# Block-sparse attention and a low-rank mixer on one core: another written-out order of steps, a refilled prologue, and w2 loaded around the values of pair 7

## The chip, the cores and the metric

The kernel runs on one core of one Trainium2 chip. The metric is the device time of one execution in microseconds (us), the median of several runs; lower is better. TensorE is called PE here, VectorE DVE, ScalarE ACT, GpSimd POOL and SyncE SP, as the profile does. DVE, ACT, POOL and SP each run their own instructions in program order, and so does PE.

## The reference: what is computed

There are two stages. The first is attention with a block mask, for 4 batches of 8 heads, 768 positions and 64 channels:

```python
scores = scale * np.matmul(q, k.transpose(0, 1, 3, 2))      # scale = 1/8
mask = np.abs(blk_i - blk_j) <= window                      # blocks of 32, window 1
mask = mask | (blk_i == 0) | (blk_j == 0) | (blk_i == n_blocks - 1) | (blk_j == n_blocks - 1)
for qb in range(n_blocks):
    for kb in sampled_blocks[qb]:                           # three random key blocks
        mask[qb * block:(qb + 1) * block, kb * block:(kb + 1) * block] = True
attn = softmax(np.where(mask, scores, -1000000000.0))
out = np.matmul(attn, v)
```

The mask is the same for all heads. The second stage takes the heads' outputs side by side as x (4 batches of 768 positions by 512 channels), mixes positions with a product of rank 32, and runs a two-layer perceptron over the channels:

```python
u = x + (x.transpose(0, 2, 1) @ U @ V).transpose(0, 2, 1)   # U 768x32, V 32x768
out = u + np.maximum(u @ w_ch1, 0.0) @ w_ch2                # 512 -> 2048 -> 512
```

## The kernel before

**Units of work.** The 32 heads are 16 pairs; pair i belongs to batch i // 4. Queries, keys and values come in as float32 and are used as 16-bit floats. A score is computed with the 128 keys of a tile as output rows and the 768 queries as columns; ACT takes the exponential of it out of PSUM into the tile `est`, with no maximum subtracted. A value product multiplies `est` by the values, which carry a column of ones, so that the sum of the exponentials comes out as a 65th column; DVE divides by it.

**Pairs 0 to 3 (batch 0).** The mask rides along in the product: `qres` and `kres` hold the 64 channels of a head and, in other rows, a one-hot code of the query's block and a row of biases for the key, so the score comes out already masked. A single score (`score`, L980) is two matmuls of 384 columns into two banks of PSUM, with an exp of 768 columns (L989); a double score (`two_scores`, L999) is four matmuls into three banks, with an exp of 1536 columns (L1007). Meanwhile PE and DVE work out the mask as an array (`mask_part`, L939), tile by tile.

**Pairs 4 to 15.** Both heads of a pair share `qpl` and `kpl`, which a DMA transposes (`front`). A quad step (`two_halves`, L1030) computes two key tiles of both heads in eight matmuls into six banks; ACT does two exps of 1536 columns (L1039), and DVE multiplies each by the mask (L1045). The value products of a head are 36 matmuls of 65 columns (L414).

**The mixer** follows a batch later, between the scores of the next batch: the products with U and V (L572 to L665), the first layer with weights `w1t` (L685), its relus on ACT (L697) or DVE (L699), and the second layer with weights `w2t` (L760). The second layer is not the plain product: it is put together from seven products of quarter size (a scheme of Strassen's kind), for which DVE forms sums of the weights (`weight_sum`, L721 or L855 and about there) and of the hidden values (`pair_sum`), and adds the products into the result (`pair_out`, L879). For the last batch both layers are done in that way (L817 to L919).

**Banks.** PSUM has eight banks. A step that writes PSUM names the bank that it takes; a step may only write a bank when the reader of what was there is done.

**The order.** Nothing is scheduled by the framework: the kernel writes the order out by hand. First comes a prologue, in plain statements. Then one long string, `PLAN`, gives a word for each step, and the loop over `PLAN.split()` emits the instructions word by word; an engine's program is what falls to it, in that order. The words that matter here:

- `S3`: a single score into banks 3 and 4; `B0`: a double score into banks 0 to 2; `Q`: a quad step into banks 0 to 5; `H`: half of one; `e`: the next exp on ACT; `p`: the mask multiply on DVE.
- `A`, `A7`: one tile of a value product, the number naming the bank where a new one begins; `V6`: all six tiles of a head; `v`: the divide on DVE; `y`: the copy behind it.
- `Z7`, `z`: PE turns the second head of pair 0, DVE copies it; `R6`, `t`: the same for queries or keys of pairs 1 to 4; `K6`, `k`: a part of the mask array and the DVE compare behind it.
- `M`, `m`, `X`, `Y`, `D`, `d`, `E`, `g`, `F`, `x`, `d.`, `T.`: the mixing with U and V; `P`, `C`, `U`, `a`, `b`: the first layer and its relus; `S.`, `H.`, `D.`: the second layer's sums, products and additions; `q.`: sums of weights.
- `t.`, `g.`, `c.`, `o.`, `r.`, `s.`, `h.`, `e.`: the two layers of the last batch, the tail of the kernel.
- `L.n`: the loads of a later pair, from `loads(n + 1)`.

**The prologue.** Two loads of pair 0's first head go out; PE runs eight matmuls of 512 columns on a constant (`keep_warm`, L272), whose result nobody reads; DVE casts the queries and works out a small array `bias` from the sampled blocks; PE turns queries and keys (`first_turn`, L227) and multiplies out the two halves of the mask rows (`mask_half`, L279); DVE and ACT copy them into `qres` and `kres` (`mask_row` L287, `first_row` L293). Then POOL casts the second head and clears some tiles, and the first transfers of pairs 0 and 1, of U, of the second set of mask rows (`second_set`) and of V are issued.

**The loads.** `loads(i)` issues, on SP, the transposes of pair i + 1 (`front`), and, on POOL, in transfers that convert to 16 bits, the queries and keys of pair i + 2 (`load_qk`) and then its values (`load_v`), two transfers for each tensor of a pair from pair 6 on (L139). The earlier pairs come through SP's queue as float32 and are cast by POOL or, in pair 0, by DVE too. w2 comes in four quarters of four row blocks (`load_w2`, L372): two behind the values of pair 6, in `loads(4)`, and two behind those of pair 7, in `loads(5)`.

The functions that the diff touches, and those that call them:

Of the kernel before, what the change touches and what calls it, by code (L numbers as in the profile page):

```python
# [23 lines left out]
def kernel(  # L24
# [167 lines left out]
    def second_set():  # L192
        for h in range(2):
            one_hot(1, h)
            nc.sync.dma_start(out=kres[1][mrows[h], h, :], in_=kres[0][mrows[h], h, :])
        nc.sync.dma_start(out=kmask[mrows[0], :], in_=kres[0][mrows[0], 0, :])

    def load_mix_u():
        uld = ldpool.tile([P, T, R], FP32, tag="ldu", name="uld", bufs=1)
        nc.sync.dma_start(out=uld, in_=moe_U.rearrange("(p t) r -> p t r", t=T))  # L200
        nc.gpsimd.tensor_copy(out=Ut[:, :, 0:R], in_=uld)

# [30 lines left out]

    with tc.manual_schedule(
# [41 lines left out]
        pks = [bank(2, [P, HS], FP32), bank(7, [P, HS], FP32)]  # L276
# [23 lines left out]
        keep_warm(8)  # L300
# [28 lines left out]
        mask_row(0, 1, nc.vector.tensor_copy)  # L329
        mask_row(1, 1, nc.vector.tensor_copy)  # L330
# [3 lines left out]
        for tile_ in (Vt, kmask):  # L334
            nc.gpsimd.memset(tile_.bitcast(FP32), 0.0)
        nc.vector.memset(Ut, 0.0)
# [3 lines left out]
        load_mix_u()  # L340
        second_set()
# [107 lines left out]
    S0 S3 e e S5 B0 e Z7 e S3 z Z6 e z A7 A B0 e R6 S3 t A R5 e A B0 t A K6 e A S3 k v A5 A e K6 k B0 A  # L449
    A e K7 A K6 k S3 k A K7 e v B0 k S3 e M6 e A5 A m R7 A t B0 K6 R3 e k A A t S6 A e v S0 D2 S3 e d A7  # L450
    A e A S0 K6 A e S3 k K2 A e S5 k A e v S3 R2 e S5 t S0 e M7 e S3 m D2 e B5 d A0 D1 e A A d A S3 D2 A
    e d K1 S5 k R7 e S3 t A S1 e v A5 A e A S3 S6 e K2 A e A k A S3 v B0 e K7 M6 e k S3 m X5 K7 e A6 Y k
    A B0 y X7 Y e S3 y E5 A e A g A R7 S0 t A e v S4 S2 e A7 A e R1 E6 A t A g A A Q v e e M6 X7 m Y P6
    y p H U7 e p H b C e p H b U7 e p H b U6 e p E1 a g p V7 Q v e e V6 U7 v p U0 a P1 b C p P6 a C E7 Q
    a g U6 e e U7 b P6 b p U0 C a U7 p a Q b X6 Y e e P7 y C P6 b C p U0 b a p V7 L.5 Q v U.0.1.3.6 e
    q.3.0 V7 a.0.1.3.0 e U.0.1.1.1 v U.0.1.11.0 a.0.1.1.1 U.0.1.5.6 q.3.1 a.0.1.11.1 p Q a.0.1.5.1 p
    U.0.1.10.6 e U.0.1.7.7 a.0.1.10.0 e U.0.1.2.6 a.0.1.7.0 S.0.0.1.3 U.0.1.9.7 p a.0.1.2.1 Q a.0.1.9.1
    q.7.1 U.0.1.4.6 e S.0.0.2.0 H.0.0.1.0.7 p H.0.0.1.1 a.0.1.4.1 U.0.1.0.0 p L.6 e U.0.1.14.1 q.4.1 V6
    a.0.1.0.1 p a.0.1.14.1 Q v q.4.0 e V6 D.0.0.0 S.0.0.3 H.0.0.6.0 e v U.0.1.13.2 q.7.0 H.0.0.6.1
    U.0.1.12.6 a.0.1.13.1 D.0.0.2 y p Q a.0.1.12.1 q.5.1 H.0.0.7.0 e H.0.0.7.1 q.5.0 H.0.0.5.0.6 D.0.0.3  # L460
    H.0.0.5.1 e S.0.0.4.4 U.0.1.6.1 p H.0.0.4.0 a.0.1.6.1 H.0.0.4.1 D.0.0.4 Q D.0.0.5 p H.0.0.3.0 e L.7
    H.0.0.3.1 p H.0.0.2.0.7 H.0.0.2.1 e p U.0.1.8.2 U.0.1.15.0 D.0.0.1 D.0.0.6 a.0.1.8.1 V7 p a.0.1.15.1
    S.0.1.1.1 Q S.0.2.1.0 V6 e v S.0.1.2.4 H.0.1.1.0.7 y v H.0.1.1.1 y H.0.1.2.0.0 S.0.2.2.3 y H.0.1.2.1
    e D.0.1.0 M6 D.0.1.1 H.0.2.1.0.1 m H.0.2.1.1 S.0.2.3 F.1.0.2.4 D.0.2.0 F.1.1.3.6 F.1.2.5.0 x.6.0
    H.0.2.6.0 x.6.1 d.6.0 H.0.2.6.1 x.7.0 d.6.1 F.1.3.6.4 D.0.2.2 H.0.1.6.0 T.6 x.5.1 H.0.1.6.1 S.0.1.3
    H.0.2.7.0 H.0.2.7.1 x.4.0 H.0.2.5.0.6 x.5.0 H.0.2.2.0.0 D.0.2.3 d.5.0 H.0.2.2.1 x.4.1 d.5.1
    H.0.2.4.0 D.0.1.2 d.4.0 T.5 x.7.1 H.0.2.4.1 d.7.0 H.0.1.7.0 D.0.2.1 d.4.1 D.0.2.5 H.0.1.7.1 d.7.1
    S.0.2.4.2 T.4 Q D.0.1.3 H.0.2.5.1 e H.0.1.4.0 T.7 D.0.2.4 H.0.1.4.1 H.0.2.3.0 e D.0.1.5 H.0.2.3.1
    Z.0.0.1 p H.0.1.5.0.7 Z.0.2.1 H.0.1.5.1 D.0.2.6 Q Z.0.2.0 D.0.1.4 Z.0.0.0 S.0.1.4.0 U.1.0.0.6 e
    H.0.1.3.0 a.1.0.0.0 H.0.1.3.1 e U.1.0.11.6 D.0.1.6 p U.1.0.10.0 Z.0.1.0 Z.0.1.1 a.1.0.11.1 U.1.0.9.7  # L470
    p L.8 a.1.0.10.1 U.1.0.6.6 a.1.0.9.1 p Q a.1.0.6.1 p U.1.0.12.6 e V7 e U.1.0.2.2 v U.1.0.5.0 p
    a.1.0.12.1 U.1.0.1.7 a.1.0.5.1 a.1.0.2.1 U.1.0.3.6 a.1.0.1.0 p Q a.1.0.3.1 V6 p e U.1.0.4.7 v e
    U.1.1.5.2 a.1.0.4.0 U.1.0.15.6 p a.1.1.5.1 U.1.1.9.7 a.1.0.15.1 p Q a.1.1.9.1 U.1.1.3.7 e L.9
    U.1.0.7.6 a.1.1.3.0 e U.1.0.14.7 a.1.0.7.0 p U.1.1.4.0 U.1.1.10.6 a.1.0.14.1 a.1.1.4.0 U.1.1.1.7 p
    a.1.1.10.1 Q a.1.1.1.1 V7 e V6 v e U.1.1.7.7 v Q a.1.1.7.1 p U.1.0.8.7 e H.1.0.1.0.6 a.1.0.8.0
    H.1.0.1.1 p e U.1.1.13.7 p U.1.0.13.0 U.1.1.14.2 p a.1.0.13.1 a.1.1.13.1 U.1.1.8.3 S.1.0.1.3
    a.1.1.14.1 U.1.1.6.7 a.1.1.8.1 S.1.0.3 Q a.1.1.6.1 S.1.0.2.0 H.1.0.2.0.7 e D.1.0.0 L.10 H.1.0.2.1
    S.1.0.4.4 H.1.0.6.0 D.1.0.1 H.1.0.6.1 e U.1.1.15.1 U.1.1.11.0 a.1.1.15.0 U.1.1.0.7 p a.1.1.11.1 Q
    D.1.0.2 a.1.1.0.1 p y V7 e H.1.0.7.0 v e H.1.0.7.1 U.1.1.2.0 p U.1.1.12.7 D.1.0.3 a.1.1.2.1 p Q
    a.1.1.12.1 S.1.1.1.0 H.1.0.4.0 e H.1.0.4.1 S.1.1.2.1 V7 D.1.0.5 e S.1.1.3 H.1.1.1.0.6 p H.1.1.1.1 Q  # L480
    D.1.1.0 v H.1.1.6.0 e L.11 p H.1.1.6.1 H.1.0.5.0.7 D.1.1.2 H.1.0.5.1 e p H.1.1.7.0 H.1.1.7.1 D.1.0.4
    V0 y p y y H.1.1.5.0.3 S.1.1.4.3 y V4 y D.1.1.3 v H.1.1.5.1 v y H.1.1.4.0 H.1.1.4.1 S.1.2.1.1 y
    H.1.0.3.0 D.1.1.4 M4 S.1.2.2.0 H.1.0.3.1 m D.1.1.5 F.2.0.5.4 F.2.1.0.1 D.1.0.6 Z.1.1.1 H.1.2.1.0.6
    x.8.0 H.1.2.1.1 x.10.0 d.8.0 H.1.1.3.0 x.10.1 d.10.0 F.2.2.7.5 D.1.2.0 F.2.3.4.2 d.10.1 H.1.2.2.0.1
# [699 lines left out]
```

## Time and profile before

| what | us |
|---|---|
| median of three runs | 270.56 |
| the three runs | 269.94, 271.41, 270.56 |
| the profiled execution, its own time | 270.01 |
| its span in the profile | 268.2 |
| first exp on ACT | 6.54 |
| first exp of a quad step (pair 4) | 43.61 |
| w2's four transfers issued | 49.40, 50.14, 58.69, 62.78 |
| w2's four transfers landed | 58.41, 62.50, 71.13, 74.54 |

The page of the profile shows one execution. Its first lines give, for each engine, the time that it was busy, the share of the span and the number of instructions; PEld is the loading of weights, which runs beside the matmuls. A table by stretch gives the same for pieces of the span, and with it the TensorE clock that was granted (1.00 is full), the busy share of the DMA engines, and GB/s. A timeline lists the instructions of an engine in order of time, those alike put together: the start, the busy time, the engine, the line and the operation, out<-in with shapes, the count; a bracket at the end holds the idle time before it and what ended it. The chain of waits goes back from the last instruction to what released it, step by step, and gives the share of the span that falls to each engine. Times in a timeline are counted from the start of the span.

### The profile page before, as it was taken

Reading aid. Unit: us, or ns where it says so; the run is one execution under the profiler, and the core shown is the slowest. Engines: PE = TensorE matmul, PEld = TensorE weight load, DVE = VectorE, ACT = ScalarE, POOL = GpSimd, SP = SyncE. Lnnn points to the kernel's source line nnn. Section 1 sums busy time; section 2 is a strip of 40 time slices with the busy share of each in tenths; the row PEclk is TensorE's granted clock in tenths of the full one; section 3 lists DMA queues with packets and bytes.
Section 4 is the critical chain, followed back from the end, with each engine's and each line's share of the span. In section 5 each row is a group of like instructions: output and inputs, shape, how many; then the busy total and the mean of one; then the engine's idle time right before and its main releaser. Section 6 shows DMA issues by size and latency. Waiting matters only on the chain.

```text
span 268.2 us, 7303 instructions
## 1 busy us (share of the span) xinstructions
PE 262.4 (98%) x3006; PEld 182.4 (68%) x3006; DVE 232.5 (87%) x477; ACT 202.7 (76%) x265; POOL 72.7 (27%) x98
## 2 busy tenths in 40 slices
PE   8899999999999999999999999999999999999995
PEld 3677775555577778565666887555667788666884
DVE  5789988988999998868588997688998999999993
ACT  4999998897989667788898857788997944789200
POOL 4669006944462570070606160000000000000000
PEclk9999999999999999999999999999999999999999
DMA  6799997999999999897938997610200116400024
GB/s 192 245 324 263 207 235 123 113 135 144 189 146 133 117 103 111 284 98 89 90 39 67 106 109 139 223 34 13 51 0 2 42 42 117 159 2 0 2 98 137
DMA packets 88720, 31.66 MB, mean 118 GB/s; under 512 B 77104, under 2 KB 85840, under 8 KB 88688
## 3 DMA queue, kind: packets, MB, share of 16 engines
q0 software_dynamic: 49728, 10.10, 48.4%
q1 hardware_dynamic: 38492, 20.86, 33.6%
q8 instruction: 23, 0.38, 0.6%
q10 hardware_dynamic: 468, 0.26, 0.4%
q14 instruction: 9, 0.07, 0.1%
HBM read 27.67 MB, written 6.29 MB: 127 GB/s over the span
## 4 chain that ended last, share of the span: by engine, by line
PE 73%; DMA 12%; DVE 7%; ACT 2%; POOL 2%; issue 1%; SPq 0%; DVEq 0%; POOLq 0%; ACTq 0%
PE ps L760 32%; PE ps L685 17%; DMA w2t<-in_moe_w_ch_dram 9%; PE ps L414 9%; PE ps L1030 7%; DMA vld<-in_v_dram 2%; PE ps L999 2%; ACT est L1007 2%; PE ps L980 1%; DVE est L1045 1%; PE ps L272 1%; DMA qpl<-stqld 1%; PE ps L665 1%; DVE xf L551 1%; DVE res L969 1%
## 5 line engine op out<-in xcount | busy, mean ns | idle before, releaser
L1039 ACT ACTIVATE est<-ps 128x1536 f16<-128x1536 f32 x72 | 100.6, 1450 | 18.8 <-PE ps L1030 18.7
L685 PE MATMUL ps<-uT,w1t 128*128 128x384 f16 x384 | 70.2, 326 | 0.0
L1045 DVE TENSOR_TENSOR est<-est,mask 128x1440 f16<-128x1440 f16 x72 | 63.4, 903 | 0.6 <-ACT est L1039 0.2
L685 PEld LDWEIGHTS <-w1t 128*128 128x128 f16 x384 | 35.6, 97 | 26.6 <-issue 6.8
L414 PEld LDWEIGHTS <-est 128*128 128x128 f16 x1152 | 40.4, 97 | 7.0 <-issue 3.3
L414 PE MATMUL ps<-vt,est 128*128 128x65 f16 x1152 | 43.3, 193 | 0.2 <-DVE xf L551 0.2
L760 PEld LDWEIGHTS <-hid 128*128 128x128 f16 x358 | 34.0, 98 | 6.6 <-issue 1.6
L697 ACT ACTIVATE hid<-ps 128x384 f16<-128x384 f32 x63 | 29.7, 496 | 4.8 <-PE ps L685 4.3
L1030 PE MATMUL ps<-qpl,kpl 64*128 64x512 f16 (+1 forms) x288 | 31.7, 325 | 0.0
L139 POOL DMA_DIRECT2D stqld<-in_q_dram x20 | 16.3, 820 | 55.9 <-DMA qpl<-stqld 54.4
L760 PE MATMUL ps<-w2t,hid 128*128 128x256 f16 x238 | 31.1, 273 | 0.0
L879 DVE TENSOR_TENSOR xf<-xf,ps 128x256 f32<-128x256 f32 x63 | 25.4, 416 | 4.1 <-PE ps L760 3.7
L699 DVE TENSOR_SCALAR hid<-ps 128x384 f16<-128x384 f32 x33 | 18.3, 555 | 8.7 <-PE ps L685 8.0
L760 PEld LDWEIGHTS <-sums 128*128 128x128 f16 x216 | 20.1, 98 | 4.4 <-issue 1.0
L989 ACT ACTIVATE est<-ps 128x768 f16<-128x768 f32 x30 | 22.5, 812 | 0.1
L1030 PEld LDWEIGHTS <-kpl 64*128 64x128 f16 x288 | 12.3, 94 | 14.3 <-issue 9.1
L760 PE MATMUL ps<-res,sums 128*128 128x256 f16 x144 | 19.4, 273 | 0.0
L634 ACT CAST xh<-xf 128x384 f16<-128x384 f32 x24 | 11.0, 510 | 10.0 <-DVE xf L630 10.0
L551 DVE TENSOR_TENSOR xf<-ps,rcp 128x384 f32<-128x384 f32 x32 | 17.7, 554 | 0.8
L139 POOL DMA_DIRECT2D stkld<-in_k_dram x20 | 16.3, 819 | 1.9 <-issue 0.8
L139 POOL DMA_DIRECT2D vt<-in_v_dram x20 | 16.3, 820 | 0.0
L760 PE MATMUL ps<-res,hid 128*128 128x256 f16 x120 | 15.9, 273 | 0.0
(121 smaller groups left out, 339.3 us busy)
## 6 DMA issues: line engine op xcount, KB each, us to landing
out_dram<-xf SPq DMA_DIRECT2D x18, 256.0 KB, 2.4
vld<-in_v_dram SPq DMA_DIRECT2D x6, 384.0 KB, 6.3
w1t<-in_moe_w_ch_dram POOLq DMA_DIRECT2D x4, 512.0 KB, 8.3
w2t<-in_moe_w_ch_dram POOLq DMA_DIRECT2D x4, 512.0 KB, 12.1
qld<-in_q_dram SPq DMA_DIRECT2D x5, 384.0 KB, 3.7
kld<-in_k_dram SPq DMA_DIRECT2D x5, 384.0 KB
stqld<-in_q_dram POOLq DMA_DIRECT2D x20, 96.0 KB, 3.9
stkld<-in_k_dram POOLq DMA_DIRECT2D x20, 96.0 KB, 4.2
```

The lines of the kernel that those rows point to most:

```text
L139: nc.gpsimd.dma_start(out=dst[:, h], in_=src[b, 2 * hp + h].rearrange("(p t) d -> p t d", t=T),)
L414: nc.tensor.matmul(pav[:, sc, :], est[:, n, sc * P : (sc + 1) * P], vts[b % 2][:, 2 * hp + h, g, 0 : D + 1], start=(g == 0 and sc == 0), s ...
L551: nc.vector.tensor_tensor(out=dst, in0=pav[:, :, 0:D], in1=rcp[:, :, None].broadcast_to([P, T, D]), op=ALU.mult,)
L685: nc.tensor.matmul(pt, w1t[:, cc, jj * P : (jj + 1) * P], bts[b].uT[:, cc, c * HS : (c + 1) * HS], start=(cc == 0), stop=(cc == NCC - 1), ...
L697: nc.scalar.activation(out=dst, in_=pt, func=AF.Relu)
L699: nc.vector.tensor_scalar_max(out=dst, in0=pt, scalar1=0.0)
L760: nc.tensor.matmul(acc[key], lhsT, rhs, start=(first and i == 0), stop=(i == len(pairs_) - 1), skip_group_check=True,)
L879: nc.vector.tensor_add(out=x, in0=x, in1=acc[a, b, tau])
L989: lambda: nc.scalar.activation(out=dst, in_=ps, func=AF.Exp, scale=0.125),
L1030: nc.tensor.matmul(units[h][:, u * S + lo : u * S + hi], kT[drows[h], g * P : (g + 1) * P], qT[drows[h], lo:hi], start=True, stop=True, sk ...
L1039: nc.scalar.activation(out=both[h], in_=units[h].rearrange("p (g n) -> p g n", g=2), func=AF.Exp, scale=0.125,)
L1045: lambda: nc.vector.tensor_mul(out=masked(both[h]), in0=masked(both[h]), in1=masked(mask[:, 2 * j : 2 * j + 2, :]),),
```

## The change

There are three parts.

**The prologue.** `keep_warm` runs seven matmuls of 512 columns and one of 256, not eight of 512; three fillers of 128 columns are added, one ahead of the first mask step and two at the prologue's end. `first_turn` takes both halves of the turned tile as weights (128 columns, not 64), for which POOL sets the half that no load has filled to 1. A part of the first key turn's copy goes from ACT to DVE, the whole of the second key turn's from DVE to ACT. The second half of the mask, its three copies, the second set of rows and the load of V leave the prologue for a new word, `W7`, at the head of the list, where one of its rows' copies that ACT did is done by DVE. Some clearing of tiles moves on POOL, and that of `Ut` goes from DVE to POOL.

**The list.** `PLAN` is another list of the same steps: each kind of word is there as often as before, save for `W7`, each kind's own sequence is the same (for the dotted words of the mixer and the tail, their order is not), the relus are split between ACT and DVE in the same numbers, and many bank numbers differ.

**w2.** Its first half is issued behind the queries and keys of pair 7, its second behind that pair's values; `loads(0)` moves from the start of pair 0 to that of pair 1.

```diff
     def second_set():
         for h in range(2):
-            one_hot(1, h)
             nc.sync.dma_start(out=kres[1][mrows[h], h, :], in_=kres[0][mrows[h], h, :])
-        nc.sync.dma_start(out=kmask[mrows[0], :], in_=kres[0][mrows[0], 0, :])
+            if h == 0:
+                nc.sync.dma_start(out=kmask[mrows[0], :], in_=kres[0][mrows[0], 0, :])
...
-                pt[0:D, j * P : (j + 1) * P],
-                sts[0, ("qld", "kld")[n]][:, 3 * c + j, 0],
+                pt[:, j * P : (j + 1) * P],
+                sts[0, ("qld", "kld")[n]][:, 3 * c + j].rearrange("p h d -> p (h d)"),
...
+        for nm in ("qld", "kld"):
+            nc.gpsimd.memset(sts[0, nm][:, :, 1], 1.0)
         for tile_ in (qres[1], kres[1]):
             nc.gpsimd.memset(tile_.bitcast(FP32), 0.0)
-        for vt in vts:
-            nc.gpsimd.memset(vt[:, :, :, D : D + 1], 1.0)
...
-        pks = [bank(2, [P, HS], FP32), bank(7, [P, HS], FP32)]
+        pks = [bank(2, [P, HS], FP32)]
...
-        keep_warm(8)
+        keep_warm(7)
+        keep_warm(1, 256)
...
         first_row(0, 1, nc.scalar.copy)
+        keep_warm(1, P)
         first_cast(0, 1, nc.vector.tensor_copy)
         mask_half(0)
         mask_row(0, 0, nc.vector.tensor_copy, 0, P)
-        mask_row(1, 0, nc.scalar.copy)
         first_turn(1, 0)
         first_row(1, 0, nc.vector.tensor_copy, 0, P)
-        first_row(1, 0, nc.scalar.copy, P, HS)
         mask_row(0, 0, nc.vector.tensor_copy, P, HS)
+        first_row(1, 0, nc.vector.tensor_copy, P, HS)
         first_turn(1, 1)
-        first_row(1, 1, nc.vector.tensor_copy)
-        mask_half(1)
-        mask_row(0, 1, nc.vector.tensor_copy)
-        mask_row(1, 1, nc.vector.tensor_copy)
+        first_row(1, 1, nc.scalar.copy)
+        keep_warm(2, P)
...
+        for h in range(2):
+            one_hot(1, h)
+
+    def late_masks(n):
+        pks.append(bank(n, [P, HS], FP32))
+        mask_half(1)
+        for h, c in ((0, 1), (1, 0), (1, 1)):
+            mask_row(h, c, nc.vector.tensor_copy)
         second_set()
         load_mix_v()
...
     PLAN = """
-    S0 S3 e e S5 B0 e Z7 e S3 z Z6 e z A7 A B0 e R6 S3 t A R5 e A B0 t A K6 e A S3 k v A5 A e K6 k B0 A
+    W7 S0 S5 e e S3 B0 Z6 z Z5 z e e S6 B3 S1 e e e R6 t A7 A A A A A v B0 e K3 k A5 R6 A A K7 S3 e t B0 e
...
-    e d K1 S5 k R7 e S3 t A S1 e v A5 A e A S3 S6 e K2 A e A k A S3 v B0 e K7 M6 e k S3 m X5 K7 e A6 Y k
+    K1 k S5 e R7 t v S3 e S1 e A5 A A S3 S6 e K2 k A A A S3 e B0 e e v M7 m K6 k K5 k S3 e X7 Y y A6 A B0 X5
...
-    y p H U7 e p H b C e p H b U7 e p H b U6 e p E1 a g p V7 Q v e e V6 U7 v p U0 a P1 b C p P6 a C E7 Q
+    H C b p e p H U7 b e p H e U6 a E2 g V7 Q e e p v V6 v U7 a U0 b P1 C P6 C a a p p E7 g Q e e U6 b U7 P6
...
             load_qk(i + 2)
+            if i == HP + 1:
+                load_w2(range(0, NJJ // 2, 4))
             load_v(i + 2)
             if i == 1:
                 load_w1(range(NCC))
-        if i in (HP, HP + 1):
-            load_w2(range((i - HP) * NJJ // 2, (i - HP + 1) * NJJ // 2, 4))
+        if i == HP + 1:
+            load_w2(range(NJJ // 2, NJJ, 4))
...
-        for m in {0: (0,), 1: (1, 2), 3: (3,), 4: (4,)}.get(i, ()):
+        for m in {1: (0, 1, 2), 3: (3,), 4: (4,)}.get(i, ()):
             loads(m)
...
+        "W": ((late_masks,) for _ in range(1)),
```

More of the change, by code (lines that the diff above doesn't have):

```diff
@@ L320 @@
         mask_row(0, 0, nc.vector.tensor_copy, 0, P)
-        mask_row(1, 0, nc.scalar.copy)
         first_turn(1, 0)
         first_row(1, 0, nc.vector.tensor_copy, 0, P)
-        first_row(1, 0, nc.scalar.copy, P, HS)
         mask_row(0, 0, nc.vector.tensor_copy, P, HS)
+        first_row(1, 0, nc.vector.tensor_copy, P, HS)
         first_turn(1, 1)
-        first_row(1, 1, nc.vector.tensor_copy)
-        mask_half(1)
-        mask_row(0, 1, nc.vector.tensor_copy)
-        mask_row(1, 1, nc.vector.tensor_copy)
+        first_row(1, 1, nc.scalar.copy)
+        keep_warm(2, P)
         for n in range(2):
             first_cast(1, n, nc.gpsimd.tensor_copy)
-        for tile_ in (Vt, kmask):
-            nc.gpsimd.memset(tile_.bitcast(FP32), 0.0)
-        nc.vector.memset(Ut, 0.0)
+        for vt in vts:
+            nc.gpsimd.memset(vt[:, :, :, D : D + 1], 1.0)
+        nc.gpsimd.memset(kmask.bitcast(FP32), 0.0)
         load_v(0)
@@ L459 @@
[L459 to L478, printed above, removed]
@@ new lines @@
+    p p D.1.0.0 p U.1.1.8.7 a.1.1.8.1 U.1.0.13.1 a.1.0.13.1 S.1.0.1.3 S.1.0.2.0 S.1.0.4.4 U.1.1.14.2
+    a.1.1.14.1 U.1.1.13.5 a.1.1.13.1 U.1.1.6.7 a.1.1.6.1 Q e L.9 L.10 H.1.0.2.0.7 H.1.0.2.1 S.1.0.3
+    H.1.0.6.0 H.1.0.6.1 D.1.0.1 U.1.1.15.0 a.1.1.15.0 e p D.1.0.2 p U.1.1.11.1 a.1.1.11.1 U.1.1.0.7
+    a.1.1.0.1 Q e e V7 v y H.1.0.7.1 H.1.0.7.0 D.1.0.3 U.1.1.2.2 a.1.1.2.1 p p U.1.1.12.7 a.1.1.12.1
+    S.1.1.1.0 S.1.1.2.1 Q e e H.1.0.4.0 H.1.0.4.1 D.1.0.5 V7 S.1.1.3 p H.1.1.1.0.6 H.1.1.1.1 D.1.1.0 Q L.11
@@ new lines @@
+    U.2.0.10.6 a.2.0.10.0 p U.2.1.4.7 a.2.1.4.1 Q e e V7 v y U.2.1.0.6 a.2.1.0.0 U.2.1.2.1 a.2.1.2.0
+    U.2.0.1.7 a.2.0.1.1 U.2.0.13.6 a.2.0.13.1 Q e e p p U.2.1.9.7 a.2.1.9.0 U.2.0.7.6 a.2.0.7.0 U.2.0.6.7
+    a.2.0.6.1 U.2.0.14.6 a.2.0.14.1 L.12 L.13 Q e e p p V7 p V6 v y v U.2.0.3.7 a.2.0.3.1 S.2.0.1.4
+    S.2.0.2.1 Q e e U.2.1.5.6 a.2.1.5.0 S.2.0.3 H.2.0.1.0.7 H.2.0.1.1 D.2.0.0 U.2.1.14.0 a.2.1.14.1 y
+    U.2.1.10.1 a.2.1.10.0 p p p U.2.1.3.6 a.2.1.3.1 Q e e H.2.0.6.0 H.2.0.2.0.6 H.2.0.6.1 D.2.0.2 H.2.0.2.1
@@ L529 @@
+    e.2.6.1 e.2.6.0
     """
```

122 lines of the change are left out of this document (65 added, 57 removed).

## The prediction

> **What bounds the kernel now.** I read the page's sums first: TensorE is busy for nearly the whole span, and the chain of waits runs mostly through it.
>
> ```profile
> span 268.2 us, 7303 instructions
> PE 262.4 (98%) x3006; PEld 182.4 (68%) x3006; DVE 232.5 (87%) x477; ACT 202.7 (76%) x265; POOL 72.7 (27%) x98
> PE 73%; DMA 12%; DVE 7%; ACT 2%; POOL 2%; issue 1%; SPq 0%; DVEq 0%; POOLq 0%; ACTq 0%
> ```
>
> An average over the span hides the stages, so the second view is the table by stretch (busy us of PE, PEld, DVE, ACT and POOL, each with its instructions, then the granted clock).
>
> ```profile
> 6.50:43.60 37.10, 35.76 (x507) 26.14 (x507) 32.22 (x72) 34.21 (x39) 18.18 (x25) 1.00 0.96 246
> 52.20:80.00 27.80, 27.56 (x317) 17.05 (x317) 25.49 (x45) 22.94 (x27) 13.71 (x18) 1.00 1.79 154
> 80.00:206.00 126.00, 125.97 (x1529) 87.40 (x1525) 107.48 (x201) 101.06 (x123) 30.34 (x38) 1.00 0.87 97
> 228.00:265.00 37.00, 37.00 (x285) 27.57 (x282) 34.29 (x94) 18.90 (x41) 0.00 (x0) 1.00 0.17 61
> ```
>
> From 80 on PE idles 0.03 us in 126 and, in the tail, nothing at all: no order of steps can win there while the work is the same. Up to about 52 it is ScalarE: in its timeline each exp follows the last, except where a bracket shows idle time.
>
> ```profile
> 6.54 2.23 ACT L989 ACTIVATE est<-ps 128x768 f16<-128x768 f32 x3
> 8.68 1.45 ACT L1007 ACTIVATE est<-ps 128x1536 f16<-128x1536 f32 x1
> 10.03 0.81 ACT L989 ACTIVATE est<-ps 128x768 f16<-128x768 f32 x1
> 11.22 1.45 ACT L1007 ACTIVATE est<-ps 128x1536 f16<-128x1536 f32 x1 [0.39 <-PE ps L999]
> 12.57 0.81 ACT L989 ACTIVATE est<-ps 128x768 f16<-128x768 f32 x1
> 13.57 1.45 ACT L1007 ACTIVATE est<-ps 128x1536 f16<-128x1536 f32 x1 [0.20 <-PE ps L999]
> ...
> 43.61 8.16 ACT L1039 ACTIVATE est<-ps 128x1536 f16<-128x1536 f32 x6 [1.20 <-PE ps L1030]
> ```
>
> Starts are 0.71 us apart behind a 768-column exp, 1.35 behind a 1536-column one. The wait for L999 comes to 1.66 us in six gaps (0.39, 0.20, 0.20, 0.26, 0.26, 0.35): a double score written to banks 0–2 cannot begin before the double exp that reads them has ended. The 1.20 before 43.61 is the first quad score behind the last exp of pair 3; both lists have it. Last, the stretch in which w2 arrives:
>
> ```profile
> 74.63 0.69 DVE L721 TENSOR_TENSOR w2t<-w2t 128x1024 f16<-128x1024 f16 x1 [0.24 <-DMA w2t<-in_moe_w_ch_dram]
> 79.73 1.25 PE L414 MATMUL ps<-vt,est 128*128 128x65 f16 x36 [0.24 <-DVE xf L551]
> 49.40 1.52 POOL L372 DMA_DIRECT2D w2t<-in_moe_w_ch_dram  x2
> 58.69 0.75 POOL L372 DMA_DIRECT2D w2t<-in_moe_w_ch_dram  x1 [2.95 <-DMA w2t<-in_moe_w_ch_dram]
> 62.78 0.74 POOL L372 DMA_DIRECT2D w2t<-in_moe_w_ch_dram  x1 [3.34 <-DMA w2t<-in_moe_w_ch_dram]
> ```
>
> POOL issues the third quarter of w2 only when the first has landed (58.41), the fourth when the second has (62.50); the fourth lands at 74.54, and one weight sum on DVE waits 0.24 for it. PE's longest gap between two streams there is 0.40, just ahead of 79.73 (by the bracket 0.24, a divide on DVE).
>
> My base is the profiled execution: 270.01 us, its span 268.2 and 1.8 around it. It is 0.55 below the median of the runs, 270.56; I add my sum to the median.
>
> **The change, part by part.** The kinds and counts of the work are the same in both lists (48 A, 30 S, 9 B, 34 Q, 126 H with dots, 84 h, 63 relus on ScalarE and 33 on DVE). What changes is the prologue, the neighbours of each step, the bank numbers, and w2's place in POOL's queue.
>
> *Prologue.* The warming row is eight matmuls of 512 columns from 0.78 to 4.14, 427 ns each. Half of one goes: the first query turn moves from 4.28 to 4.07. The row of bias is ready at 4.46 either way, the mask matmul moves from 4.98 to about 4.86, the DVE copies behind it (0.29 and 0.28) end at 5.83, not 5.95, and the first exp moves from 6.54 to about 6.45: −0.1. The fillers of 128 columns (about 0.1 or less each) stand where PE waits for DVE. Turns with 128 weight columns instead of 64 cost nothing: the loads lie under the matmuls, and PEld rows of 128 columns (97 ns) are no longer than the present ones (0.60 for six). Against this, DVE now copies a 256-column mask row (0.42) and key row (ScalarE took 0.36) in front of the second score, so the second exp moves from 7.26 to about 7.33. The second half of the mask (one matmul and three copies of 0.42 to 0.57, so some 1.65 us of DVE) moves behind the prologue: it lies ahead of DVE's copies z, t and v, and PE waits for those only where banks or turned rows are short. The two memsets on POOL lie ahead of casts at 5.79 which wait 3.18 for their DMA: hidden. The transfers of one_hot and kmask go to SP's queue in another order, with 10 us and more before they are read. Sum at the second exp: +0.07.
>
> *Stage 1.* The order of the exps is the same, so only gaps count. The double score of head (0,1), keys 0 and 1, now goes to banks 3–5, and waits for a DVE copy (z) at about 9.92, not for the double exp before it: exp 6 starts at 10.83, not 11.22 (−0.39). But the next score uses banks 1 and 2, and the next double score, on 0–2, then follows directly behind its exp: that exp ends about 12.94, the four matmuls and the latency take 0.7, and exp 8 starts at 13.65 (before 13.57, +0.08): a gap of 0.76 where there was 0.20. Exp 9's score now stands behind six PE steps (two K of 0.16, three A of 0.33, an R of 0.35): 15.2 against 14.92 (+0.28). By the same addition exp 10 is +0.09, exp 11 +0.21, exp 12 +0.03, exp 14 0, exp 16 +0.07. Two later places cost again: a score on bank 0 behind a product (+0.2), a double score of pair 2 behind copies (+0.25 in all). At the first quad exp (43.61) I carry +0.2. What the old gaps give is given back at new ones.
>
> *w2.* Its first half is issued behind the queries and keys of pair 7 (at about 52.6 and 53.4 instead of 49.40 and 50.14), its second behind v, at about 55.8 and 56.6 instead of 58.69 and 62.78, since eight other issues of pair 7 now stand between the halves. The first half took 9.0 and 12.4 us to land: 62 and 66, before the first weight sum that reads it (66.9, not moved in the list). The second half took 12.4 and 11.8: 69 to 74 by the traffic beside it. So the 0.24 of DVE and most of PE's 0.40 at 79 go. They are worth little: behind them two relus now both stand on ScalarE ahead of the next quad's exp, and by adding the steps the quad after comes at 83.15, not 83.09. Sum: 0, bounded by −0.4 (the stall goes, nothing comes) and +0.5 (one relu of 0.50 late). The queries and keys of pair 7 are no longer behind two w2 issues (1.52), which gives their transposes (landed 75.0 and 77.05, read at 78.67) that much more room.
>
> *The rest.* Same matmuls, packed PE: it can only lose. Where a new neighbour waits for DVE, I counted its slack: a product of pair 8 0.25, a second-layer step behind its relu 0.5, the first steps of the tail 0.2, its first token sum 2.5. DVE is busy 34.29 of 37 us there, so slack is small. I take +0.1; bounds 0 and +0.6.
>
> Sum: +0.2 to the first quad, 0 for w2, +0.1 for the rest: +0.3, so 270.3 for the profiled execution, and on the median 270.56 + 0.24 = **270.8**.
>
> *The clock.* The granted clock reads 1.00 throughout, yet in the prologue 128-column turns take 106 ns until about 5.2 and 55 behind that. The sum takes the turning point as fixed. The Trainium skill (TensorE: Matmul & The Clock Gate, section What's actually happening) speaks against that: the gate opens after about 3.4 us of activity by a window that runs freely, so its place differs from run to run. By that rule, the shorter warming row with its gap could move it; the trace of one execution shows only the one place.
>
> **The rivals.**
>
> *A, faster:* the new gaps don't come. PE has 1.34 us of idle in 37.1 there, DVE nearly five, so the copies may be early enough; all six gaps (1.66) go, with 0.1 at the start and 0.3 at the w2 stall. About −2.0: 268.5. For it: the bank of exp 6 is really free earlier. Against it: exp 8's direct succession on banks 1–2 is in the list whatever DVE does.
>
> *B, slower:* the late mask. DVE's 1.65 us of mask copies, now between z, t and v, hold bank after bank: scores on a bank that DVE or an exp has just read (exps 8, 9, and one each in pairs 1 and 2) wait 0.3 to 0.8 each, as the 0.39 and the 0.76 above. It decides when DVE's backlog outlasts PE's own fill between two scores (about 1.0 us). Four such come to 1.2 to 3.2, less what the old gaps give (0.4 to 0.9): +1.6, 272.2, within 271.9 to 272.9.
>
> *C, the clock:* it turns later. Six key turns (6 × 0.05), the mask (0.16) and the first score (2 × 0.16) at half speed: +0.8 at most, 271.2 to 271.6.
>
> *D:* the w2 move does nothing, since PE hides it: that is nearly my forecast (0 of the sum).
>
> **How the numbers follow.** Forecast (with D) 0.47, A 0.18, B 0.27, C 0.08. A measurement of this kernel tells about 0.5% (1.35 us) from no change: below 269.2 is faster, above 271.9 slower. A gives faster 0.18; the forecast's own spread (the bounds of w2 and the rest, 270.1 to 271.6) and most of C lie within; B and the ends of both give slower 0.31. The range takes in A's value and B's: 268.5 to 272.8.
>
> **What would show it.** In ScalarE's timeline: first exp at 6.45, second at 7.33, the double exp at 10.83 without its 0.39, a gap of about 0.8 ahead of the next double exp, the first quad exp at 43.8. A start there below 42.5 means A, above 45 B. In the transfers: the last quarter of w2 landed before 74, the weight sum without its wait, no PE stall at 79. From 80 on PE must stay packed; idle of over 0.5 us there, or in the tail, breaks the forecast. Key turns of 106 ns mean C.

## The result, and the profile after

| what | before | changed |
|---|---|---|
| median of eight runs each, us | 270.44 | 273.17 |
| lowest and highest, us | 269.94, 272.20 | 272.04, 273.56 |
| ratio, 95% interval | 1 | 1.0087 (1.0060 to 1.0114) |
| profiled execution, its span, us | 268.2 | 270.5 |

A ratio here is that of the means of the runs, with two runs of the kernel before that fell in a slower state of the chip left out. The change makes the kernel slower by 0.87%, some 2.35 us on 270.44 (the medians are 2.73 apart). The forecast was no change, 270.8, in a range from 268.5 to 272.8: by the ratio the changed kernel comes to 272.8 on 270.44, at the upper end of that range, and its median, 273.17, lies above it. The first lines of the page, to be held against those of before:

```profile
span 270.5 us, 7316 instructions
PE 262.1 (97%) x3009; PEld 181.2 (67%) x3009; DVE 232.4 (86%) x477; ACT 202.6 (75%) x264; POOL 74.0 (27%) x101
```

PE is busy for as long as before (262.1, 262.4), in a span that is 2.3 longer: the time is idle time of PE, and it is not spread out. The table by stretch (PE, PEld, DVE, ACT and POOL) says where:

```profile
6.50:43.60 37.10, 35.79 (x506) 25.56 (x507) 31.13 (x69) 34.36 (x39) 18.85 (x28) 1.00 0.92 244
52.20:80.00 27.80, 27.80 (x316) 17.19 (x314) 25.76 (x46) 22.95 (x28) 16.09 (x21) 1.00 1.81 165
80.00:206.00 126.00, 123.94 (x1486) 85.58 (x1484) 105.91 (x196) 101.66 (x126) 29.40 (x37) 1.00 0.83 95
```

The first stage has lost next to nothing, 52 to 80 has gained its 0.24, and from 80 to 206, where PE had idled 0.03 us, it now idles 2.06. The view of PE's waits from 52 on has two lines (it had one, of 0.2):

```profile
PE ps L691 <- DMA uT<-xh: 1.2, 1, 1.2
PE ps L423 <- DVE xf L557: 0.9, 1, 0.9
```

Held against before quad by quad (the start of each quad's first exp), the changed kernel is at +0.12 at the first quad, −0.19 from pair 7 to 118.94, +0.74 at the next quad, +1.90 from 174.07 on, and +2.3 at the end.

**The first stall.** The chain of waits around it (start, time, what):

```profile
113.68 4.25 DMA out_dram<-xf
117.94 0.10 DVE rcp L550
118.04 1.04 issue
...
119.18 0.57 DVE xf L557
119.75 0.04 issue
119.79 1.25 PE ps L423 x36
```

PE has finished a quad at 118.91 and wants the second head's products of pair 8, in the bank that the first head's result still holds. DVE has the reciprocal at 117.94, then stands for 1.04 us, put down to nothing ("issue"), and divides at 119.18. What it writes is the float32 result `xf`, of which there are two buffers: batch 2 takes the one of batch 0, which six stores read. In the changed list the store of row 0 comes last; it is issued at 113.68, and its packets go beside 128-byte packets of a later pair's loads. Nearly all have ended at 117.44, and four more end between 118.04 and 118.52: the first of them starts at 117.80, as a packet of 16 KB of instructions ends (116.84, 0.96 us). A transfer reports its end in sixteen completions (the profile counts 16 transfer engines). For this store fifteen of them have come by 117.79, the sixteenth comes at 119.00, and the divide starts 0.18 later: that is what DVE waits for. In the list before, all six stores had been issued by 111.8, and the last completion had come at 113.86. SP's timeline, before and changed:

```profile
107.36 4.47 SPq L707 DMA_DIRECT2D out_dram<-xf  x6
...
112.14 2.05 SPq L713 DMA_DIRECT2D out_dram<-xf  x4
```

**The second stall.** The same view 46 us later:

```profile
166.33 4.39 DMA uT<-xh
170.72 0.04 issue
170.76 0.32 PE ps L691
```

The first layer of batch 2 needs the transposed mixing result `uT` of all four pairs. SP issues the transposes of pairs 8 and 10 at 161.23, then two stores of 256 KB (163.83, 1.04 us), and only then pairs 9 and 11; the last starts at 166.33 and lands 4.39 later. Before, the four stood in a row, the last at 165.3, and landed 2.8 later. SP's timeline, before and changed:

```profile
161.03 5.54 SPq L623 DMA_TRANSPOSE uT<-xh  x4
...
161.23 2.55 SPq L629 DMA_TRANSPOSE uT<-xh  x2
163.83 1.04 SPq L713 DMA_DIRECT2D out_dram<-xf  x2
164.98 2.60 SPq L629 DMA_TRANSPOSE uT<-xh  x2
```

Here too fifteen of the sixteen completions are early: they have come by 169.16, before PE wants the tile at about 169.4, though 1.1 later than all sixteen before (168.09). The sixteenth comes at 170.72, and again a packet of 16 KB of instructions lies in between (168.70, 0.93 us; before, it ran at 169.52, behind the transposes). Of the packets of 4 bytes that close the transpose, 30 have run by 168.62 and the last two start at 169.62, as the instructions end. So the two stores cost the transposes their margin, and the wait itself is that one late completion.

**What came as forecast.** ScalarE's timeline in stage 1:

```profile
6.45 2.41 ACT L995 ACTIVATE est<-ps 128x768 f16<-128x768 f32 x3 [0.59 <-PE ps L986]
10.77 1.48 ACT L1013 ACTIVATE est<-ps 128x1536 f16<-128x1536 f32 x1
13.63 1.45 ACT L1013 ACTIVATE est<-ps 128x1536 f16<-128x1536 f32 x1 [0.68 <-PE ps L1005]
15.16 0.81 ACT L995 ACTIVATE est<-ps 128x768 f16<-128x768 f32 x1
43.73 8.16 ACT L1045 ACTIVATE est<-ps 128x1536 f16<-128x1536 f32 x6 [1.25 <-DVE xh L557]
```

The bracket of 0.39 before the second double exp has gone, one of 0.68 stands before the third: 10.83, 13.65, 15.2 and 43.8 had been forecast.

**What looked as forecast and was not.** The start at 6.45 has another cause. In the prologue (two PE lines of before, then the changed kernel):

```profile
4.98 0.33 PE L279 MATMUL ps<-res,bias 24*128 24x384 f16 x1
6.01 0.50 PE L980 MATMUL ps<-res 128*128 128x384 f16 x2
...
4.41 0.49 PE L281 MATMUL ps<-res,bias 24*128 24x384 f16 x2
4.78 0.76 DVE L289 CAST res<-ps 24x128 f16<-24x128 f32 x2 [0.17 <-PE ps L281]
5.57 0.28 DVE L295 CAST res<-ps 64x128 f16<-64x128 f32 x1
5.91 0.50 PE L986 MATMUL ps<-res 128*128 128x384 f16 x2 [0.45 <-DVE res L295]
```

Line 281 (279 before) is the mask matmul, and there are two of them ahead of the key turns; one of the two DVE copies on line 289 is a mask row of 384 columns. The step `W7` stands at the head of the list, outside the prologue's block of statements, and in the kernel as built its matmul and its first copy have moved up in front of the key rows. From the first mask matmul to the first score it takes 1.50 us, against 1.03 before. What hid this is the clock: in this execution the matmuls run at full speed from 3.92 on, before from 4.83.

### The profile page after: what moved, and what is told of

It is laid out like the page before. It is cut to its first block, busy times and chain, and to the rows that moved or that the text cites. A ratio compares the mean times of both kernels' runs of the same rounds, so it can differ in the third digit from the quotient of the medians.

```text
span 270.5 us, 7316 instructions
## 1 busy us (share of the span) xinstructions
PE 262.1 (97%) x3009; PEld 181.2 (67%) x3009; DVE 232.4 (86%) x477; ACT 202.6 (75%) x264; POOL 74.0 (27%) x101
## 4 chain that ended last, share of the span: by engine, by line
PE 86%; ACT 4%; DVE 4%; DMA 3%; issue 1%; SPq 0%; DVEq 0%; ACTq 0%
PE ps L766 32%; PE ps L691 22%; PE ps L423 12%; PE ps L1036 10%; PE ps L986 3%; ACT est L1013 2%; DMA uT<-xh 2%; PE ps L1005 2%; DMA out_dram<-xf 2%; ACT est L995 1%; PE ps L274 1%; PE ps L671 1%; DVE xf L925 1%; PE ps L959 1%; DVE est L1051 1%
## 5 line engine op out<-in xcount | busy, mean ns | idle before, releaser
L1051 DVE TENSOR_TENSOR est<-est,mask 128x1440 f16<-128x1440 f16 x72 | 62.6, 901 | 1.0 <-ACT est L1045 0.9
L423 PEld LDWEIGHTS <-est 128*128 128x128 f16 x1152 | 39.2, 97 | 7.3 <-issue 4.6
L423 PE MATMUL ps<-vt,est 128*128 128x65 f16 x1152 | 41.6, 193 | 0.9 <-DVE xf L557 0.9
L139 POOL DMA_DIRECT2D stqld<-in_q_dram x20 | 16.3, 821 | 56.8 <-DMA qpl<-stqld 56.6
```

The costliest lines, as they stand in the source:

```text
L139: nc.gpsimd.dma_start(out=dst[:, h], in_=src[b, 2 * hp + h].rearrange("(p t) d -> p t d", t=T),)
L423: nc.tensor.matmul(pav[:, sc, :], est[:, n, sc * P : (sc + 1) * P], vts[b % 2][:, 2 * hp + h, g, 0 : D + 1], start=(g == 0 and sc == 0), s ...
L1051: lambda: nc.vector.tensor_mul(out=masked(both[h]), in0=masked(both[h]), in1=masked(mask[:, 2 * j : 2 * j + 2, :]),),
```

## The experiments

The theory after the result: two stalls of about 0.9 and 1.2 us, both from the place of stores in SP's queue, a third loss from the mask copy, and a small one at the end. The rivals for the stalls are that the products of pair 8 stand too close (first) and that ScalarE's casts or the exps beside them set the transposes (second). Ratios are to the kernel before, run on the same chip, with the 95% interval. Twelve kernels were run, on four chips: those of e1 to e3 on one, e4, e6, before_w2_moved and old_head on a second, e21, old_prologue and the changed kernel's repeat on a third. A stall's length below is the bracket in PE's timeline: 0.88 and 1.18 in the changed kernel.

**Three stores of batch 0 earlier** (e1_stores_early).

```diff
-    ... D.0.1.4 Z.0.1.1 S.0.1.4.0 Q Z.0.2.1 L.8 e e
+    ... D.0.1.4 Z.0.0.0 Z.0.0.1 Z.0.2.0 Z.0.1.1 S.0.1.4.0 Q Z.0.2.1 L.8 e e
-    ... D.0.1.6 Z.0.1.0 Z.0.0.1 Z.0.2.0 U.1.0.11.6 ... Q e e Z.0.0.0 v y V7
+    ... D.0.1.6 Z.0.1.0 U.1.0.11.6 ... Q e e v y V7
```

> The changed kernel, with three of batch 0's stores (rows 0, 1 and 4, complete long before) put in front of the store of row 3, so ahead of pair 10's transposes on SP; nothing else moves. Theory (the divide of pair 8's first head writes the buffer that batch 0's last store still reads): the divide moves from 119.18 to about 118.1, PE's stall at 118.5 falls from 1.04 to 0.2 or less, the quad exps of pair 9 and on come 0.8 to 1.0 earlier, the span goes from 270.5 to about 269.6 (ratio to before about 1.005). Rival (the two products of pair 8 stand too close, and the divide is late by itself): the divide stays at 119.2 or moves by less than 0.3, span 270.2 or more.

Measured: 272.09, ratio 1.0071 (1.0048 to 1.0094). DVE around the divide:

```profile
118.51 0.19 DVE L550 RECIPROCAL rcp<-ps 128x6 f32<-128x6 f32 x1
118.73 0.56 DVE L557 TENSOR_TENSOR xf<-ps,rcp 128x384 f32<-128x384 f32 x1
```

The divide now follows its reciprocal at once (0.22 from start to start, 1.32 in the changed kernel), PE has no stall over 0.1 there, and the next quad's lag grows by 0.06 where it grew by 0.93. The theory holds for the stall. The span did not fall as forecast, 270.3 for 269.6: this execution started later (first quad at 44.39, not 43.73, with the same prologue).

**Two stores of batch 1 behind the transposes** (e2_stores_behind).

```diff
-    d.10.1 d.10.0 T.10 Z.1.0.0 Z.1.1.1 H.1.2.1.0.6 ...
+    d.10.1 d.10.0 T.10 H.1.2.1.0.6 ...
-    ... Q e e T.9 p T.11 U.2.0.4.6
+    ... Q e e T.9 p T.11 Z.1.0.0 Z.1.1.1 U.2.0.4.6
```

> The changed kernel, with two stores of batch 1 (rows 0 and 3) moved behind the transposes of pairs 9 and 11 on SP; nothing else moves. Theory (the two stores stand in front of the last transposes, in SP's queue and in the transfer): the last transposes are issued about 0.7 earlier and land near 168.9 instead of 170.72, PE's stall at 169.25 goes from 1.35 to 0.3 or less, span about 269.4 (ratio about 1.004). Rival (the casts on ACT, or the exps beside them, set the transposes' start): they start at 164.9 and 166.3 as now, the stall stays over 1.0, span 270.3.

Measured: 271.32, ratio 1.0042 (1.0020 to 1.0065), span 269.4. On SP the four transposes stand together again, and PE runs on into the first layer without a bracket:

```profile
161.40 5.53 SPq L629 DMA_TRANSPOSE uT<-xh  x4
167.03 5.04 SPq L713 DMA_DIRECT2D out_dram<-xf  x5
```

The stall has gone, and the first one is still there (0.74). The rival falls.

**The same two stores through POOL** (e2_stores_pool).

```diff
-        nc.sync.dma_start(
+        queue = nc.gpsimd if (b, row) in ((1, 0), (1, 3)) else nc.sync
+        queue.dma_start(
             out=out[b].rearrange("(p t) d -> p t d", t=T)[:, row, :],
```

> The changed kernel, with the same two stores left in their place but issued by POOL, which has nothing to do there. If it is SP's time of issue (two stores take 1.04) that delays the transposes: they are issued 0.7 earlier and PE's stall falls to 0.6 or less. If it is the stores' bytes in front of the transposes in the transfer engines: the issue is earlier, but the last landing and the stall stay within 0.3 of 170.7 and 1.35.

Measured: 278.55, ratio 1.0306 (1.0274 to 1.0339), against both expectations. POOL did have work there: its next loads (six transfers of a later pair) stood behind the two stores, which waited 12.09 us for the additions.

```profile
159.81 1.13 POOL L714 DMA_DIRECT2D out_dram<-xf  x2 [12.09 <-DVE xf L886]
171.99 0.48 PE L691 MATMUL ps<-uT,w1t 128*128 128x384 f16 x2 [2.95 <-DMA uT<-xh]
174.22 0.48 PE L691 MATMUL ps<-uT,w1t 128*128 128x384 f16 x1 [1.75 <-DMA uT<-xh]
```

The loads, in packets of 128 bytes, now ran beside the transposes' packets of 256, and PE stalled for 2.95 and 1.75. So this run doesn't tell SP's time of issue from the bytes in front of the transposes. The other traces do: from its issue to its fifteenth completion the last transpose took 2.83 in the changed kernel, 2.78 with the stores behind it and 2.73 before, while its issue was 0.99 later in the changed kernel than before. It is the issue.

**Both moves of stores** (e3_both). The two diffs together (the transposes also stand earlier in the list, which leaves SP's program as it is).

> The changed kernel with both moves of stores. Theory: both stalls go, 2.0 to 2.3 in all: span 268.2 to 268.6, ratio to before 0.999 to 1.003. Rival (new waits come in their place, DVE or another store): ratio over 1.005.

Measured: 270.79, ratio 1.0012 (0.9997 to 1.0028). Both stalls are gone, as expected, and with them most of the loss. Its profiled execution has a span of 270.1, for a reason of its own. The table by stretch, cut where the granted clock changes (it is the 1.00 or 0.50 ahead of the DMA share and GB/s):

```profile
3.89:7.31 3.42, 2.34 (x22) 1.16 (x21) 3.10 (x11) 1.77 (x4) 1.20 (x5) 1.00 0.91 262
7.31:10.72 3.41, 3.41 (x18) 2.08 (x19) 0.83 (x3) 2.63 (x4) 2.19 (x5) 0.50 0.95 326
```

The clock opened at 3.89, fell back to half at 7.31, and opened again 3.41 later; the first quad comes 38.7 behind the first exp, not 37.3, a loss of 1.4.

**The mask step back in the prologue** (e4_mask_in). On top of both moves:

```diff
-    def late_masks(n):
-        pks.append(bank(n, [P, HS], FP32))
+        pks.append(bank(7, [P, HS], FP32))
         mask_half(1)
...
-    W7 S0 S5 e e S3 B0 ...
+    S0 S5 e e S3 B0 ...
```

> The changed kernel with both moves of stores, and the step W7 put back as the prologue's last statements, so that the second mask matmul and its copies really come behind the key rows. Theory (in the changed kernel this matmul and one copy of 384 columns run ahead of the key turns, and the copy of 0.47 stands on DVE in front of the key row): from the start of the first mask matmul to the first score 1.0 instead of 1.5, the time about 0.5 below the kernel with the two moves alone, ratio to before 0.998 to 1.000. Rival (the first score waits for something else, or only the clock's phase differs): still 1.5, ratio 1.001.

Measured: 270.43, ratio 1.0000 (0.9975 to 1.0025), 0.36 below the kernel with both moves. The two ran on different chips (against each one's own kernel before, the medians differ by 0.29) and their intervals overlap, so a gain in time is not clear of noise; what is shown is the order. It is as the theory has it: one mask matmul, the key turns, the other one.

```profile
4.97 0.33 PE L281 MATMUL ps<-res,bias 24*128 24x384 f16 x1
5.34 0.29 DVE L289 CAST res<-ps 24x128 f16<-24x128 f32 x1 [0.15 <-PE ps L281]
5.70 0.28 DVE L295 CAST res<-ps 64x128 f16<-64x128 f32 x1
5.87 0.33 PE L281 MATMUL ps<-res,bias 24*128 24x384 f16 x1
6.13 0.50 PE L985 MATMUL ps<-res 128*128 128x384 f16 x2
```

From the mask matmul to the first score it is 1.16, and 1.07 in the next kernel, against 1.5: the distance is the copy's. What moves the step up when it stands outside the block is open; that its place decides is shown. In this execution the first quad comes 38.1 behind the first exp, with the clock open all the time: PE waits 0.68 at 11.84 for POOL's cast of queries and 0.48 at 14.57 for the transfer of `kmask`, which SP had issued at 8.93.

**The last four steps as before** (e6_tail_end). The product in halves last, then its two additions in their old order:

```diff
-    ... e.1.6 h.2.3.3.8 h.2.3.2 e.2.6.1 e.2.6.0
+    ... e.1.6 h.2.3.2 h.2.3.3.8 e.2.6.0 e.2.6.1
```

> The kernel of e4_mask_in with the last four steps in the order of before (the product that is split into halves last, then its two additions). Theory: the last addition ends 0.2 earlier behind the last matmul and the last store goes out by ACT's queue; 0.2 to 0.3 less than e4_mask_in from the last quad to the end. Rival (the end is the store's own time): no difference of over 0.1.

Measured: 270.38, ratio 1.0005 (0.9991 to 1.0018). From the end of the last addition to the end of the span 3.00, as without it (2.70 before): the rival holds, this is not the cause.

**w2's loads alone, on the kernel before** (before_w2_moved). The diff of `loads` given above, and nothing else.

> The kernel before, with only w2's loads moved as in the change. Theory (the weight sum no longer waits for w2's last quarter, and the stall of 0.40 at 79 goes): last quarter landed before 73, quads of pair 7 from the second on 0.2 to 0.3 earlier, ratio 0.999. Rival (in the changed kernel it is the other order of steps that takes the stall away): the wait of 0.24 goes, but the second quad of pair 7 stays within 0.1, ratio 1.000. A slower result would be a wait of the first weight sums.

Measured: 270.14, ratio 0.9989 (0.9974 to 1.0004), which is not clear of no change. DVE's wait for w2 is gone. The quads of pair 7 come 0.11 earlier against the six before them (in the changed kernel 0.24): nearly half is w2's, the rest is the order.

**The head of before, the rest of the change** (old_head). The prologue and the list of before up to the products of pair 5, then the changed list with both moves, the old last four steps and w2 moved.

> The prologue and the list of before up to the products of pair 5, and from there the list, w2's place and the ends of e6_tail_end. Theory (the new order of stage 1 gives back at new gaps what it saves): within 0.3 of e6_tail_end. Rival (the new order of stage 1 is itself slower, or is faster once the mask copy is out of the way): a difference of over 0.4 at the first quad exp, where the clock opens at the same time.

Measured: 269.96, ratio 0.9989 (0.9978 to 1.0000). It is 0.42 below e6_tail_end by the medians, more than the theory's 0.3; at the first quad, where the rival wanted over 0.4, the two differ by 0.19 counted from the first exp. Its middle part gains: quads 0.45 ahead of before from pair 13 on.

**The old prologue alone** (old_prologue). The prologue of before with the whole list of e6_tail_end.

> The prologue of before, and behind it the whole list of e6_tail_end (stage 1 too). If the prologue (256 columns less of warming, the DVE copies) makes the difference of 0.42 between e6_tail_end and old_head: the time is that of old_head, within 0.15, 269.9 to 270.1. If the order of stage 1 makes it: the first quad exp comes 37.3 behind the first exp instead of 37.05, and the time is 270.2 to 270.4. Both can hold in parts.

Measured: 270.56, ratio 1.0009 (0.9987 to 1.0030). The first quad comes 37.40 behind the first exp, 37.25 in e6_tail_end, 37.29 in the changed kernel; with the old list it is 37.07 before, 37.05 in old_head, 37.18 in e21_early, but 37.55 in before_w2_moved, where PE waits 0.76 at 10.17 for POOL's cast of values. So the order of stage 1 costs about the 0.2 that was forecast, no more than such executions differ. The time is above both of those expected, and no better than with the new prologue and the mask put in, so no gain of the old prologue by itself shows, and the 0.42 stays open.

**One addition of the tail earlier** (e21_early). On old_head, `e.2.1` two steps behind its last matmul.

> The kernel of old_head with one addition of the tail (second product sum of row 2, which a store of 128 KB follows) two steps behind its last matmul, as in the list before, instead of 2.5 us later among the last stores. Theory (one store too many stands in SP's queue and in the transfer at the end): from the end of the last addition to the end of the span 2.7 instead of 3.0; span 267.8, ratio 0.998. Rival (the last store's own time): 3.0 as now.

Measured: 270.64, ratio 1.0019 (1.0003 to 1.0034), a miss. DVE ran into a wait for that matmul, a token sum behind it came late, and PE stalled for 0.46 at 261.3; from the last addition to the end 2.94.

**Another addition of the tail earlier** (e16_early). On old_head, the products and the addition of row 1 four matmuls earlier.

```diff
-    h.1.4.0 h.1.4.3 e.1.5 h.2.3.1 h.1.3.2 h.1.3.3 e.1.6 h.2.3.2
+    h.1.3.2 h.1.3.3 e.1.6 h.1.4.0 h.1.4.3 e.1.5 h.2.3.1 h.2.3.2
```

> The kernel of old_head with two products and the addition of row 1 that ends in a store of 128 KB moved four matmuls earlier in the last microseconds, so that this store is not the one right in front of the last two; the additions before it stay in place. Theory (the store ahead of the last ones takes the 0.3, on SP and in the transfer): from the end of the last addition to the end of the span 2.7 instead of 3.0, no stall of the matmuls; span 267.8, ratio 0.998. Rival (something else at the end): 3.0 as in old_head, ratio 0.999.

Measured: 270.13, ratio 0.9978 (0.9958 to 0.9999). The 0.3 at the end stays (3.12), so the theory fails there. By its interval this version is a little faster than before, by 0.2% (by the medians, 270.13 and 270.33, 0.07%); old_head, from which it differs only by the place of these words, has 0.9989, and the two intervals overlap.

**The changed kernel once more** (changed_again).

> The changed kernel as it is, beside the others on one chip. The sum of the causes: 0.5 for the mask copy ahead of the key row, 0.9 and 1.2 for the two stalls, 0.3 at the end, 0.2 for stage 1, less 0.3 for the weight sums: 2.8 over before, ratio 1.009 to 1.011. The stalls of 1.0 and 1.35 stay; the first score stands 1.5 behind the first mask matmul whatever the clock does.

Measured: 272.72, ratio 1.0085 (1.0058 to 1.0111), a little short of the sum of the causes. The first score stands 1.49 behind the first mask matmul, as expected. In its profiled execution the clock fell back just as in e3_both, from 7.29 to 10.71; PE had been busy 2.23 of the 3.41 us before.

```profile
3.88:7.29 3.41, 2.23 (x21) 1.15 (x19) 2.74 (x11) 1.67 (x4) 0.60 (x2) 1.00 0.85 269
```

The second stall is there with 1.00, the first is not: the divide at 120.16 follows its reciprocal by 0.35. The stores stand in the same places, two microseconds later like everything else, and all their packets have ended at 119.65; the packet of instructions comes only at 120.49. The store's last completion is at 119.98, only 0.16 behind the fifteenth. In e2_stores_behind, where the stall was 0.74, that packet ran at 116.74, amid the store; fifteen completions had come by 118.08, the sixteenth at 119.16. In all three the divide starts 0.17 or 0.18 behind the last completion. So the first stall needs both: the store issued last, and something that holds up its last packets.

The second stall shows the same. In e1_stores_early fifteen completions of the last transpose come by 168.87, the sixteenth at 170.46, with the packet of instructions at 168.39; here the packet runs at 169.34, amid the transpose, whose last packets end at 170.81 and whose completions come from 171.45 on. In the kernels without the stalls the two transfers had ended or nearly ended when that packet came. That the packet holds them up fits the times in all these executions; no run moved the packet alone. By the medians, taking the first stall away is worth 0.53 (271.32 to 270.79), the second 1.30 (272.09 to 270.79).

## Why the prediction was right or wrong

- **Prologue, forecast −0.1 at the first exp and +0.07 at the second: wrong, though 6.45 was met to the hundredth.** The working took the statements' order for the instructions' order. The second mask matmul and a copy of 0.47 ran ahead of the key row, which costs 0.47 on the way to the first score (1.50 for 1.03), and the clock, open 0.9 earlier in that one execution, gave it back; the second exp, at 7.35 for 7.33, was met by the same luck. In other executions of this prologue the first exp is at 6.65, 6.86, 6.94, 7.08 and 7.14. By the medians the copy is worth 0.3 to 0.4, which is not clear of noise. "10 us and more before they are read" was wrong for `kmask`: SP issues it at 9.03 and PE reads it at 13.4, and in e4_mask_in PE waited for it.
- **Stage 1, forecast +0.2 to the first quad: right, step by step.** Exps 6, 8 and 9 at 10.77, 13.63 and 15.16; from the first exp to the first quad 37.29 for 37.07. What the old gaps gave was given back. Rival A falls with this. Of rival B the waits for a bank just read are there (0.68, 0.16, 0.26 and 0.32 ahead of double exps, 1.42 in all for 1.66 before), but not the pile-up behind the mask copies: the first quad stands at 43.73, not above 45.
- **w2, forecast 0: right in kind, small in size.** The wait of 0.24 and the stall went; −0.24 at pair 7, of which −0.11 is w2's alone. The forecast's relus, which were to give it all back, didn't. The later issue times were not those worked out (58.23 and 59.70 for 55.8 and 56.6): POOL waited for the transfers of queries instead of those of w2. Two issues stand between the halves, the values of pair 7, and not eight; the landings came as forecast all the same (62.8, 65.3, 70.4 and 73.8).
- **The rest, forecast +0.1 with bounds 0 and +0.6: the step that failed.** It measured 0.93 and 1.16 by the quads, where the prediction had said that idle time of over 0.5 from 80 on breaks it (2.06 came). The sentence "a product of pair 8 0.25" counted the slack of DVE's steps alone; the divide also waits for the last store of the batch whose buffer it overwrites (in one of three executions nothing held up that store's last completion, and the wait was 0.13). The transposes ahead of the first layer were not counted at all. Both lie in SP's program, and the working had read the moved stores only as work off the path. Taking the place of the stores back removes both stalls and moves the ratio from 1.0087 to 1.0012. That the time still came out at the end of the range is luck: that end was rival B's price, for a late mask in stage 1, and the time was lost elsewhere.
- **The end, forecast 0: +0.3**, from the last addition to the end of the span (3.02 for 2.70). Three tries at its cause failed. The traces place it: the last store is issued 0.03 behind the last addition in both kernels, and its last completion comes at 1.61 before and 1.92 in the changed one, with 290 KB and 457 KB of stores moved behind that addition. The bytes alone do not explain it (e21_early has 311 KB and 1.86), so the cause stays open.
- **Rival C, the clock: it is there, in another form.** The opening is not late by the shorter row; it lies anywhere from 3.60 to 5.87 in eight executions of this prologue or its variant, 3.65 to 4.83 with the old one. But in two of them the clock fell back, at a price of 1.4, which the prediction had not thought of.

Together, in the profiled executions: −0.19 up to pair 9, 0.93, 1.10 to the last quad (the second stall of 1.16 and the order around it), and 0.47 from there to the end (0.32 of it behind the last addition): 2.31 for 2.3. That leaves the medians, 2.73 apart: the profiled execution of the changed kernel (272.32) is one of its better ones, with the clock open early.

## What to carry to other kernels

When an order of steps is changed, the queue that issues stores and transposes must be read like an engine: for each buffer used again, find the last transfer that reads it, and for each product find the last transfer that feeds it, and work out both times in the new order. A store that nobody waits for at once is waited for by the next writer of its buffer. A transfer has landed only with its last completion, and a margin smaller than the lateness of one of them (1.2 and 1.6 us here) is none. And a start that matches a forecast proves little until its parts match too.

## What the runs showed of the hardware

The granted clock went back to half for 3.41 us when PE had been busy 2.23 and 2.34 us of the 3.41 behind the opening; it stayed open after 2.41, 2.56, 2.57 and 2.72 with the same prologue, and after 2.71 to 3.02 where the mask copy was out of the way or the prologue the old one. That is no threshold of PE's busy time, though: counting windows of 3.41 on from the opening, it also stayed open after 2.23 (changed kernel, from 167.75, with the second stall), 2.20 (e1_stores_early, from 264.59) and 2.06 (e4_mask_in, from 263.78). What is counted is not shown. Between two changes of the clock lies a whole number of 3.413 us in every trace: 78 in the changed kernel (266.24 us), 77 before (262.83). The Trainium skill (TensorE: Matmul & The Clock Gate, section What's actually happening) says that the window is about 3.4 us long and runs freely, so that the place of the change differs between runs; the runs agree with it, with lengths of 3.41 and openings from 3.60 to 5.87. The section has the clock closed after an idle window; here a window two thirds busy was enough. In the kernel with two stores on POOL, one window with 0.48 us of work closed it for 6.83 us. Among the runs with a clock on record, the kernel with two stores on POOL left aside, a mean granted clock below 0.996 (the two executions with the dip have 0.991 and 0.994) was seen in 6 of 44 with the changed prologue, in none of 24 with the mask step put back, and in 4 of 158 with the old one.

In both stalls of the changed kernel a packet of 16 KB of instructions (0.96 and 0.93 us long) ran ahead of a transfer's last packets, which started as it ended, and one of the transfer's sixteen completions came 1.2 and 1.6 us later than the other fifteen.
